# Regrouping the score matmuls and the PSUM banks of a two-block attention kernel

## The chip, the cores and the metric

The kernel runs on one core of a Trainium2 chip. The metric is the time of one execution on the device in microseconds (us). A core has a matrix engine (TensorE, PE in the profile; its weight loads are PEld), a vector engine (VectorE, DVE), a scalar engine (ScalarE, ACT), GpSimd (POOL) and a queue engine that starts DMAs (SyncE, SP). Matmuls write to PSUM, which has eight banks of 128 partitions by 512 fp32 values; VectorE and ScalarE read from there into SBUF.

## What is computed

Two independent attention blocks read two inputs of 2048 tokens by 640 features, and their outputs are put side by side. Both have 32 heads of 20 features.

```python
# A: sliding window of 256 tokens, softmax
scores = einsum("bhqd,bhkd->bhqk", q, k) * Dh**-0.5
scores = where((i - j >= 0) & (i - j < 256), scores, -1e9)
a = einsum("bhqk,bhkd->bhqd", softmax(scores), v) -> [B, S, D] @ wo
# B: linear attention, phi(t) = where(t > 0, t + 1, exp(t)) + 1e-6
kv = einsum("bhsd,bhse->bhde", phi(k), v); z = sum_s phi(k)
b = (phi(q) @ kv) / (phi(q) @ z + 1e-6) -> [B, S, D] @ wo
```

## The kernel before, in words

Tokens are cut into 16 blocks of 128 (NB). The framework tracks which instruction needs which tile, gives each tile a slot of its pool when an earlier tile of the same name has let go of it, and puts the instructions of each engine in an order ahead of time, in which work that is written later may be woven in where an engine would stand idle. Once that order is made, each engine keeps it: an instruction that waits holds back all behind it on its engine.

Up to about 115 us, x is loaded and transposed, and block B sums its key-value products over the token blocks (loop at line 131), in three PSUM banks of the pool `psB` (line 130). Then A's V, Q and K are projected (lines 200 to 237) and B's phi(q) (lines 238 to 261), in the four banks of `psAP`.

The attention loop of A (lines 288 to 359) takes the heads in eight groups g of four. The four heads lie on the partitions 0, 32, 64 and 96 of `qkg`, which DMAs fill (line 294). For each key block j of a group:

- Line 334: four score matmuls (20 rows of one head, 128 keys by up to 384 queries), each on its own 32 rows of the array (`tile_position`). Two share a tile `st` of two banks; the pool `psST` has two such tiles (line 277), so the second pair of j and the first pair of j+1 each wait until the exponential that reads the tile ahead of them is done.
- Line 341: one exponential on ScalarE for each pair, 128 by 2 x 384, from `st` into `e_t` in SBUF.
- Lines 345 and 351: GpSimd sets to zero what the causal diagonal and the window's edge exclude.
- `do_pv(j - 1)`, line 301: for each of the four heads up to three matmuls (line 308) of `e_t` with V into one PSUM tile `ops`, with one bank (`psO`, line 278); the column 21 of V is ones, so the softmax's denominator comes along. VectorE takes the reciprocal (line 316) and multiplies into `O_all` (line 317).

The second half of B (lines 417 to 472) is written behind this loop, and the framework weaves it in. For each of 16 token blocks tb: 10 matmuls of phi(q) with the masked key-value matrix into two tiles `na` and `nb` (line 422); on VectorE the denominators (lines 429, 434, 439) and two products (lines 442, 448); five transposes (line 457) and their copy (line 459); ten matmuls with B's output weights into `oa` (512 wide) and `ob` (128 wide; line 464), two copies (lines 470, 471) and a store. All take their tiles from the three banks of `psB`.

Last comes A's output projection (lines 475 to 494): for each token block five transposes of `O_all` (line 479), a copy on VectorE (line 481), ten matmuls (line 486), two copies on ScalarE (lines 492, 493) and a store. It too uses the three banks of `psB`.

So the banks of the attention loop are: three of `psB`, four of `psST`, one of `psO`.

Of the kernel before, what the change touches and what calls it, by code (L numbers as in the profile page):

```python
# [8 lines left out]
F32 = mybir.dt.float32  # L9
BF16 = mybir.dt.bfloat16  # L10
ALU = mybir.AluOpType
ACTF = mybir.ActivationFunctionType


@with_exitstack
def kernel(
# [110 lines left out]
    KVacc = bc1.tile([P, KVW], F32)  # L127
    nc.vector.memset(KVacc[:], 0.0)
    pqT_all = bc1.tile([P, KC, S], BF16)
    psB = ctx.enter_context(tc.tile_pool(name="psB", bufs=3, space=bass.MemoryType.PSUM))  # L130
    for tb in range(NB):
        kps = []
        for kk, (lo, hi) in enumerate([(0, 320), (320, 640)]):
            pb = psB.tile([P, 512], F32, name="pb")
# [21 lines left out]
        v1v = V1.rearrange("p (h e) -> p h e", e=E21)  # L156
        nc.gpsimd.memset(v1v[:, :, Dh:E21], 1.0)  # L157
        for (lo, hi, h0v, h1v) in [(0, 480, 0, 24), (480, 640, 24, 32)]:
            pb = psB.tile([P, 512], F32, name="pb")
# [11 lines left out]
        kva = psB.tile([P, 512], F32, name="pb")  # L171
        kvb = psB.tile([P, 512], F32, name="pb")
# [101 lines left out]
    epool = ctx.enter_context(tc.tile_pool(name="epool", bufs=6))  # L274
    smallp = ctx.enter_context(tc.tile_pool(name="smallp", bufs=3))
    lctx = ctx.enter_context(ExitStack())
    psST = lctx.enter_context(tc.tile_pool(name="psST", bufs=2, space=bass.MemoryType.PSUM, side="right"))
    psO = lctx.enter_context(tc.tile_pool(name="psO", bufs=1, space=bass.MemoryType.PSUM, side="right"))

    def repack_segments(col):  # L280
        c0, p0 = col // P, col % P
# [3 lines left out]
            segs.append((c0 + 1, 0, Dh - n1, n1))  # L285
        return segs

    for g in range(NG):
        qkg = awork.tile([P, 2, S], BF16)
        for t in range(2):  # L290
# [8 lines left out]
        e_tiles = {}  # L299

        def do_pv(i):
            ops = psO.tile([P, 4 * E21], F32, name="ops")
            kbs = [kb for kb in range(i - 2, i + 1) if kb >= 0]
            for s in range(4):
                h = 4 * g + s
                for ii, kb in enumerate(kbs):
                    part = i - kb
                    nc.tensor.matmul(  # L308
                        ops[:, s * E21:(s + 1) * E21],
                        lhsT=e_tiles[kb][:, s, part * P:(part + 1) * P],  # L310
                        rhs=V_aug[:, kb, h * E21:(h + 1) * E21],
                        start=(ii == 0), stop=(ii == len(kbs) - 1),
                    )
# [3 lines left out]
            nc.vector.tensor_tensor(  # L317
                out=O_all[:, i, 80 * g:80 * (g + 1)].rearrange("p (s d) -> p s d", d=Dh),
                in0=ops3[:, :, 0:Dh],
                in1=rden.to_broadcast([P, 4, Dh]),  # L320
                op=ALU.mult,
            )
            if i - 2 in e_tiles:
                del e_tiles[i - 2]

        for j in range(NB):
            nqb = min(3, NB - j)
            nq = nqb * P
            e_t = epool.tile([P, 4, 3 * P], BF16)
            for pair in range(2):  # L330
                st = psST.tile([P, 2, 512], F32)
                for sl in range(2):
                    s = 2 * pair + sl
                    nc.tensor.matmul(  # L334
                        st[:, sl, 0:nq],
                        lhsT=qkg[32 * s:32 * s + Dh, 1, j * P:(j + 1) * P],
                        rhs=qkg[32 * s:32 * s + Dh, 0, j * P:j * P + nq],
                        start=True, stop=True,
                        tile_position=(32 * s, 0),
                    )  # L340
                nc.scalar.activation(  # L341
                    out=e_t[:, 2 * pair:2 * pair + 2, 0:nq], in_=st[:, :, 0:nq],
                    func=ACTF.Exp, scale=scale,
                )
            nc.gpsimd.affine_select(  # L345
                out=e_t[:, :, 0:P], in_=e_t[:, :, 0:P],
                pattern=[[0, 4], [1, P]], compare_op=ALU.is_ge, fill=0.0,
# [65 lines left out]
    for idx, (ch, bank, c0, ncol) in enumerate(num_plan):  # L413
        first_of_bank.setdefault(bank, idx)
        last_of_bank[bank] = idx

    for tb in range(NB):
        na = psB.tile([P, 512], F32, name="pb")
        nb = psB.tile([P, 512], F32, name="pb")
        ntiles = (na, nb)  # L420
        for idx, (ch, bank, c0, ncol) in enumerate(num_plan):
            nc.tensor.matmul(  # L422
                ntiles[bank][:, c0:c0 + ncol],
                lhsT=pqT_all[:, ch, tb * P:(tb + 1) * P],
                rhs=KVbd[:, ch, 512 * bank + c0:512 * bank + c0 + ncol],
                start=(idx == first_of_bank[bank]), stop=(idx == last_of_bank[bank]),
            )
        den = bw2.tile([P, H, 1], F32)
        nc.vector.tensor_scalar(
            out=den[:, 0:24, :],  # L430
            in0=na[:, 0:24 * E21].rearrange("p (h e) -> p h e", e=E21)[:, :, Dh:E21],
            scalar1=1e-6, scalar2=None, op0=ALU.add,
        )
        nc.vector.tensor_scalar(
            out=den[:, 24:32, :],
            in0=nb[:, 0:8 * E21].rearrange("p (h e) -> p h e", e=E21)[:, :, Dh:E21],
            scalar1=1e-6, scalar2=None, op0=ALU.add,
        )
        nc.vector.reciprocal(out=den[:], in_=den[:])
        o_sb = bw2.tile([P, D], BF16)  # L440
        o_v = o_sb.rearrange("p (h d) -> p h d", d=Dh)
        nc.vector.tensor_tensor(
            out=o_v[:, 0:24, :],
            in0=na[:, 0:24 * E21].rearrange("p (h e) -> p h e", e=E21)[:, :, 0:Dh],
            in1=den[:, 0:24, :].to_broadcast([P, 24, Dh]),
            op=ALU.mult,
        )
        nc.vector.tensor_tensor(
            out=o_v[:, 24:32, :],
            in0=nb[:, 0:8 * E21].rearrange("p (h e) -> p h e", e=E21)[:, :, 0:Dh],  # L450
            in1=den[:, 24:32, :].to_broadcast([P, 8, Dh]),
            op=ALU.mult,
        )
        tpsb_t = psB.tile([P, 512], F32, name="pb")
        tpsb = tpsb_t[:].bitcast(BF16).rearrange("p (c t) -> p c t", t=P)
        for c in range(KC):
            nc.tensor.transpose(tpsb[:, c, :], o_sb[:, c * P:(c + 1) * P], ident[:])  # L457
        oTb = bw2.tile([P, KC, P], BF16)
        nc.vector.tensor_copy(out=oTb[:], in_=tpsb[:, 0:KC, :])
        oa = psB.tile([P, 512], F32, name="pb")  # L460
        ob = psB.tile([P, 512], F32, name="pb")
        for (tgt, lo, hi) in [(oa, 0, 512), (ob, 512, 640)]:
            for c in range(KC):
                nc.tensor.matmul(  # L464
                    tgt[:, 0:hi - lo],
                    lhsT=oTb[:, c, :], rhs=Wo_B[:, c, lo:hi],
                    start=(c == 0), stop=(c == KC - 1),
                )
        osbB = bw2.tile([P, D], BF16)
        nc.vector.tensor_copy(out=osbB[:, 0:512], in_=oa[:, 0:512])  # L470
        nc.vector.tensor_copy(out=osbB[:, 512:640], in_=ob[:, 0:128])
        nc.sync.dma_start(out2[tb * P:(tb + 1) * P, D:2 * D], osbB[:])

    lctx.close()
    for tb in range(NB):
        tpsA_t = psB.tile([P, 512], F32, name="pb")
        tpsA = tpsA_t[:].bitcast(BF16).rearrange("p (c t) -> p c t", t=P)
        for c in range(KC):
            nc.tensor.transpose(tpsA[:, c, :], O_all[:, tb, c * P:(c + 1) * P], ident[:])
        oT = awork.tile([P, KC, P], BF16)  # L480
        nc.vector.tensor_copy(out=oT[:], in_=tpsA[:, 0:KC, :])  # L481
        opa = psB.tile([P, 512], F32, name="pb")
        opb = psB.tile([P, 512], F32, name="pb")
        for (tgt, lo, hi) in [(opa, 0, 512), (opb, 512, 640)]:
            for c in range(KC):
                nc.tensor.matmul(  # L486
# [38 lines left out]
```

## Time and profile before

| | us |
|---|---|
| median of 6 runs | 481.14 (480.25 to 481.97) |
| the profiled execution: its time | 480.25 |
| its span, first to last instruction | 478.5 |
| TensorE busy in it | 418.9 |
| ScalarE busy in it | 246.8 |
| VectorE busy in it | 228.7 |
| GpSimd busy in it | 173.0 |

The profile is of one execution. Its second part cuts the span into 40 equal slices and gives the busy share of each engine in tenths, and under PEclk the clock that TensorE was granted, in tenths of full speed. A list of groups gives, for the instructions of one line and form, the count, then the busy time and the mean of one in ns, then the time for which the engine had stood idle just before them and what ended it. The chain of waits goes back from the last instruction, at each step to what released it. Tables by stretch give, for each engine, the busy time and the number of instructions.

### The profile page before, as it was taken

How to read it: one execution, taken by the hardware profiler on the slowest of the kernel's cores; microseconds unless marked ns; L12 is line 12 of the kernel's file. 1: busy time of each engine (PE TensorE's matmuls, PEld its weight loads, DVE VectorE, ACT ScalarE, POOL GpSimd, SP SyncE). 2: the span in 40 equal slices, each digit the busy share in tenths (PEclk: the TensorE clock that was granted, in tenths of full speed). 3: DMA queues.
4: the chain of work that ended last, by engine and by line, in shares of the span. 5: the costliest groups of instructions: out<-in, count | busy, mean ns of one | idle time of the engine just before them, and what ended most of it. 6: DMA issues, size and time to landing. Idle time of an engine off the chain costs nothing.

```text
span 478.5 us, 9156 instructions
## 1 busy us (share of the span) xinstructions
PE 418.9 (88%) x3580; PEld 217.4 (45%) x3612; DVE 228.7 (48%) x635; ACT 246.8 (52%) x377; POOL 173.0 (36%) x373
## 2 busy tenths in 40 slices
PE   2299999999999495999999999999999988899775
PEld 1166666655444132444445444444444434344443
DVE  1188889887333489444444444344344422222221
ACT  0012222222223134776777777777777788777332
POOL 0010000000003920654555655656555567555000
PEclk9999999999999879555555555555555555555899
DMA  8980000000001300002102003012020020000111
GB/s 299 366 322 2 1 0 1 2 0 2 0 1 30 80 1 0 15 15 53 32 15 55 29 15 71 16 29 56 15 55 16 15 70 3 1 15 0 70 70 69
DMA packets 14154, 22.86 MB, mean 48 GB/s; under 512 B 1440, under 2 KB 11552, under 8 KB 14112
## 3 DMA queue, kind: packets, MB, share of 16 engines
q1 hardware_dynamic: 10688, 17.21, 12.2%
q10 hardware_dynamic: 3424, 5.08, 3.0%
q8 instruction: 28, 0.46, 0.4%
q14 instruction: 14, 0.11, 0.1%
HBM read 11.80 MB, written 5.24 MB: 36 GB/s over the span
## 4 chain that ended last, share of the span: by engine, by line
PE 70%; DVE 9%; ACT 8%; POOL 5%; DMA 4%; issue 3%; SPq 1%; ACTq 0%; POOLq 0%; DVEq 0%
PE st L334 17%; PE pb L464 9%; PE aps L226 9%; PE ops L308 8%; ACT e_t L341 7%; PE pb L486 5%; PE pb L136 5%; DMA Wv_A<-in_A_wqkv_dram 4%; PE aps L204 4%; PE pb L161 4%; PE pb L422 2%; PE pb L457 2%; DVE pqT_all L258 2%; DVE pqT_all L254 2%; PE pb L176 2%
## 5 line engine op out<-in xcount | busy, mean ns | idle before, releaser
L341 ACT ACTIVATE e_t<-st 128x768 bf16<-128x768 f32 (+2 forms) x256 | 191.6, 769 | 61.9 <-PE st L334 53.6
L334 PE MATMUL st<-qkg 20*128 20x384 bf16 (+2 forms) x512 | 121.9, 473 | 14.6 <-ACT e_t L341 5.0
L345 POOL TENSOR_SCALAR_AFFINE_SELECT e_t<-e_t 128x512 bf16<-128x512 bf16 x128 | 81.2, 634 | 126.1 <-ACT e_t L341 126.1
L308 PEld LDWEIGHTS <-e_t 128*128 128x128 bf16 x1440 | 60.0, 108 | 48.3 <-issue 29.7
L316 DVE RECIPROCAL rden<-ops 128x4 f32<-128x4 f32 x128 | 23.0, 180 | 115.0 <-PE ops L308 114.5
L308 PE MATMUL ops<-V_aug,e_t 128*128 128x21 bf16 x1440 | 73.3, 184 | 4.2 <-POOL e_t L351 0.9
L351 POOL TENSOR_SCALAR_AFFINE_SELECT e_t<-e_t 128x512 bf16<-128x512 bf16 x112 | 71.0, 634 | 0.0
L334 PEld LDWEIGHTS <-qkg 20*128 20x128 bf16 x512 | 27.2, 99 | 56.7 <-issue 49.5
L464 PE MATMUL pb<-Wo_B,oTb 128*128 128x512 bf16 (+1 forms) x144 | 49.8, 436 | 0.6 <-DVE O_all L317 0.3
L226 PE MATMUL aps<-xT_A,Wqk_u 128*128 128x512 bf16 x193 | 44.9, 379 | 0.4
L204 PE MATMUL aps<-Wv_A,xT_A 128*128 128x480 bf16 (+1 forms) x160 | 30.8, 305 | 9.5 <-DMA Wv_A<-in_A_wqkv_dram 8.9
L486 PE MATMUL pb<-Wo_A,oT 128*128 128x512 bf16 (+1 forms) x153 | 30.5, 330 | 7.7 <-DVE oT L481 7.3
L317 DVE TENSOR_TENSOR O_all<-ops,rden 128x80 bf16<-128x80 f32 x128 | 30.6, 239 | 3.8
L244 PE MATMUL aps<-xT_B,Wb 128*128 128x512 bf16 x98 | 26.3, 420 | 6.2 <-DVE pqT_all L254 6.0
L236 ACT CAST qkT_u<-aps 128x512 bf16<-128x512 f32 x20 | 11.7, 585 | 37.3 <-DVE qkT_u L234 37.3
L157 POOL MEMSET V<- 128x32 bf16 x16 | 3.7, 244 | 71.6 <-PE pb L176 58.3
L226 PEld LDWEIGHTS <-Wqk_u 128*128 128x128 bf16 x200 | 19.4, 98 | 21.1
L136 PE MATMUL pb<-Wb,xT_B 128*128 128x320 bf16 x160 | 26.2, 298 | 0.0
L147 ACT ACTIVATE ek<-pb 128x320 bf16<-128x320 f32 x32 | 14.0, 437 | 21.9 <-PE pb L136 21.5
L234 DVE CAST qkT_u<-aps 128x512 bf16<-128x512 f32 x20 | 13.8, 690 | 23.1 <-PE aps L226 23.1
L161 PE MATMUL pb<-Wb,xT_B 128*128 128x480 bf16 (+1 forms) x160 | 24.3, 299 | 0.0
L252 ACT ACTIVATE eqc<-aps 128x512 bf16<-128x512 f32 x20 | 11.9, 597 | 23.9 <-DVE pqT_all L254 16.1
(55 smaller groups left out, 410.4 us busy)
## 6 DMA issues: line engine op xcount, KB each, us to landing
qkg<-qkT_u SPq DMA_DIRECT2D x56, 80.0 KB
x_nat_A<-in_A_x_dram SPq DMA_DIRECT2D x4, 640.0 KB
x_nat_B<-in_B_x_dram ACTq DMA_DIRECT2D x4, 640.0 KB
out_dram<-osbB SPq DMA_DIRECT2D x16, 160.0 KB
out_dram<-osb SPq DMA_DIRECT2D x16, 160.0 KB
Wb<-in_B_wqkv_dram SPq DMA_DIRECT2D x1, 2400.0 KB
Wqk_u<-in_A_wqkv_dram ACTq DMA_DIRECT2D x1, 1600.0 KB
Wv_A<-in_A_wqkv_dram SPq DMA_DIRECT2D x1, 800.0 KB
```

The costliest lines, as they stand in the source:

```text
L136: nc.tensor.matmul(pb[:, 0:hi - lo], lhsT=xT_B[:, kc, tb * P:(tb + 1) * P], rhs=Wb[:, kc, D + lo:D + hi], start=(kc == 0), stop=(kc == KC ...
L161: nc.tensor.matmul(pb[:, 0:hi - lo], lhsT=xT_B[:, kc, tb * P:(tb + 1) * P], rhs=Wb[:, kc, 2 * D + lo:2 * D + hi], start=(kc == 0), stop=(k ...
L204: nc.tensor.matmul(vps[:, bank, 0:hi - lo], lhsT=xT_A[:, kc, kb * P:(kb + 1) * P], rhs=Wv_A[:, kc, lo:hi], start=(kc == 0), stop=(kc == KC ...
L226: nc.tensor.matmul(qps[:, k, 0:tn], lhsT=Wqk_u[:, kc, c * P:(c + 1) * P], rhs=xT_A[:, kc, ts0:ts0 + tn], start=(kc == 0), stop=(kc == KC - 1),
L308: nc.tensor.matmul(ops[:, s * E21:(s + 1) * E21], lhsT=e_tiles[kb][:, s, part * P:(part + 1) * P], rhs=V_aug[:, kb, h * E21:(h + 1) * E21] ...
L317: nc.vector.tensor_tensor(out=O_all[:, i, 80 * g:80 * (g + 1)].rearrange("p (s d) -> p s d", d=Dh), in0=ops3[:, :, 0:Dh], in1=rden.to_broa ...
L334: nc.tensor.matmul(st[:, sl, 0:nq], lhsT=qkg[32 * s:32 * s + Dh, 1, j * P:(j + 1) * P], rhs=qkg[32 * s:32 * s + Dh, 0, j * P:j * P + nq], ...
L341: nc.scalar.activation(out=e_t[:, 2 * pair:2 * pair + 2, 0:nq], in_=st[:, :, 0:nq], func=ACTF.Exp, scale=scale,)
L345: nc.gpsimd.affine_select(out=e_t[:, :, 0:P], in_=e_t[:, :, 0:P], pattern=[[0, 4], [1, P]], compare_op=ALU.is_ge, fill=0.0, base=0, channe ...
L351: nc.gpsimd.affine_select(out=e_t[:, :, 2 * P:3 * P], in_=e_t[:, :, 2 * P:3 * P], pattern=[[0, 4], [-1, P]], compare_op=ALU.is_gt, fill=0. ...
L464: nc.tensor.matmul(tgt[:, 0:hi - lo], lhsT=oTb[:, c, :], rhs=Wo_B[:, c, lo:hi], start=(c == 0), stop=(c == KC - 1),)
L486: nc.tensor.matmul(tgt[:, 0:hi - lo], lhsT=oT[:, c, :], rhs=Wo_A[:, c, lo:hi], start=(c == 0), stop=(c == KC - 1),)
```

## The change

The change regroups the attention loop and hands its eight PSUM banks out in another way:

- The score tiles become three (six banks). The two tiles of a key block are taken together and all four score matmuls are written one after the other, ahead of the two exponentials. A dependency by hand makes the first of the four wait for the first exponential of the key block before (`DEP_SYNC`); `DEP_ORDER` is defined and not used.
- `do_pv` runs two key blocks behind the scores, where it was one. Its output tile is a slot of a ring of four (`opsring`), all within one bank.
- The second half of B has one bank instead of three: the two parts of the numerators, the transposes and the two parts of the output projection each take it in turn and are evicted before the next. The reciprocal is taken for each part of the heads by itself, so there are two for each token block.
- B's first half keeps three banks, in a pool of its own that is released ahead of the attention loop.
- A's output projection gets banks of its own: four for the results, two for the transposes, in the place of the score tiles.

```diff
-    psB = ctx.enter_context(tc.tile_pool(name="psB", bufs=3, space=bass.MemoryType.PSUM))
+    psB1 = tc.alloc_tile_pool(name="psB1", bufs=3, space=bass.MemoryType.PSUM)
...
+    psB1.release()
+    psB = ctx.enter_context(tc.tile_pool(name="psB", bufs=1, space=bass.MemoryType.PSUM))
+    psO = ctx.enter_context(tc.tile_pool(name="psO", bufs=1, space=bass.MemoryType.PSUM))
...
-    psST = lctx.enter_context(tc.tile_pool(name="psST", bufs=2, space=bass.MemoryType.PSUM, side="right"))
-    psO = lctx.enter_context(tc.tile_pool(name="psO", bufs=1, space=bass.MemoryType.PSUM, side="right"))
+    psST = lctx.enter_context(tc.tile_pool(name="psST", bufs=3, space=bass.MemoryType.PSUM, side="right"))
...
+    opsring = psO.tile([P, 4, 4 * E21], F32)
+    first_exp = []
...
-            ops = psO.tile([P, 4 * E21], F32, name="ops")
+            ops = opsring[:, i % 4, :]
...
+            sts = [psST.tile([P, 2, 512], F32, name="st"), psST.tile([P, 2, 512], F32, name="st")]
+            for s in range(4):
+                mm = nc.tensor.matmul(
+                    sts[s // 2][:, s % 2, 0:nq],
+                    lhsT=qkg[32 * s:32 * s + Dh, 1, j * P:(j + 1) * P],
+                    rhs=qkg[32 * s:32 * s + Dh, 0, j * P:j * P + nq],
+                    start=True, stop=True,
+                    tile_position=(32 * s, 0),
+                )
+                if s == 0 and first_exp:
+                    tc.add_manual_dep(mm.ins, first_exp[-1].ins.name, DEP_SYNC, reason="four")
             for pair in range(2):
-                st = psST.tile([P, 2, 512], F32)
-                for sl in range(2):
-                    s = 2 * pair + sl
-                    nc.tensor.matmul(
...
+                ex = nc.scalar.activation(
+                    out=e_t[:, 2 * pair:2 * pair + 2, 0:nq], in_=sts[pair][:, :, 0:nq],
                     func=ACTF.Exp, scale=scale,
                 )
+                if pair == 0:
+                    first_exp.append(ex)
...
-            if j >= 1:
-                do_pv(j - 1)
+            if j >= 2:
+                do_pv(j - 2)
+        do_pv(NB - 2)
         do_pv(NB - 1)
...
+        for bank, (hlo, hhi) in enumerate([(0, 24), (24, 32)]):
+            nt = psB.tile([P, 512], F32, name="pb")
...
+            nc.vector.reciprocal(out=den[:, hlo:hhi, :], in_=den[:, hlo:hhi, :])
...
+        for (lo, hi) in [(0, 512), (512, 640)]:
+            opt = psB.tile([P, 512], F32, name="pb")
...
+            nc.vector.tensor_copy(out=osbB[:, lo:hi], in_=opt[:, 0:hi - lo])
...
     lctx.close()
+    psAO = ctx.enter_context(tc.tile_pool(name="psAO", bufs=4, space=bass.MemoryType.PSUM, side="right"))
+    psAT = ctx.enter_context(tc.tile_pool(name="psAT", bufs=2, space=bass.MemoryType.PSUM, side="right"))
     for tb in range(NB):
-        tpsA_t = psB.tile([P, 512], F32, name="pb")
+        tpsA_t = psAT.tile([P, 512], F32, name="pat")
...
-        opa = psB.tile([P, 512], F32, name="pb")
-        opb = psB.tile([P, 512], F32, name="pb")
+        opa = psAO.tile([P, 512], F32, name="pao")
+        opb = psAO.tile([P, 512], F32, name="pao")
```

More of the change, by code (lines that the diff above doesn't have):

```diff
@@ L12 @@
 ACTF = mybir.ActivationFunctionType
+DEP_SYNC = mybir.DependencyInfo(mybir.DependencyClass.Sync, mybir.DependencyReason.DATA)
+DEP_ORDER = mybir.DependencyInfo(mybir.DependencyClass.NoSync, mybir.DependencyReason.DATA)
 @with_exitstack
@@ L133 @@
         for kk, (lo, hi) in enumerate([(0, 320), (320, 640)]):
-            pb = psB.tile([P, 512], F32, name="pb")
+            pb = psB1.tile([P, 512], F32, name="pb")
             for kc in range(KC):
@@ L158 @@
         for (lo, hi, h0v, h1v) in [(0, 480, 0, 24), (480, 640, 24, 32)]:
-            pb = psB.tile([P, 512], F32, name="pb")
+            pb = psB1.tile([P, 512], F32, name="pb")
             for kc in range(KC):
@@ L170 @@
             )
-        kva = psB.tile([P, 512], F32, name="pb")
-        kvb = psB.tile([P, 512], F32, name="pb")
+        kva = psB1.tile([P, 512], F32, name="pb")
+        kvb = psB1.tile([P, 512], F32, name="pb")
         for ch, (h0, h1) in enumerate(chunk_heads):
@@ L329 @@
             e_t = epool.tile([P, 4, 3 * P], BF16)
-            for pair in range(2):
-                st = psST.tile([P, 2, 512], F32)
-                for sl in range(2):
-                    s = 2 * pair + sl
[L334 to L342, printed above, removed]
+            sts = [psST.tile([P, 2, 512], F32, name="st"), psST.tile([P, 2, 512], F32, name="st")]
[9 more added lines that the diff above has]
+                    tc.add_manual_dep(mm.ins, first_exp[-1].ins.name, DEP_SYNC, reason="four")
+            for pair in range(2):
+                ex = nc.scalar.activation(
+                    out=e_t[:, 2 * pair:2 * pair + 2, 0:nq], in_=sts[pair][:, :, 0:nq],
                     func=ACTF.Exp, scale=scale,
                 )
+                if pair == 0:
+                    first_exp.append(ex)
             nc.gpsimd.affine_select(
@@ L417 @@
     for tb in range(NB):
[L418 to L427, printed above, removed]
@@ L428 @@
-        den = bw2.tile([P, H, 1], F32)
[L429 to L439, printed above, removed]
+        den = bw2.tile([P, H, 1], F32)
@@ L440 @@
         o_sb = bw2.tile([P, D], BF16)
         o_v = o_sb.rearrange("p (h d) -> p h d", d=Dh)
[L442 to L453, printed above, removed]
+        for bank, (hlo, hhi) in enumerate([(0, 24), (24, 32)]):
+            nt = psB.tile([P, 512], F32, name="pb")
+            for idx, (ch, bk, c0, ncol) in enumerate(num_plan):
+                if bk != bank:
+                    continue
+                nc.tensor.matmul(
+                    nt[:, c0:c0 + ncol],
+                    lhsT=pqT_all[:, ch, tb * P:(tb + 1) * P],
+                    rhs=KVbd[:, ch, 512 * bank + c0:512 * bank + c0 + ncol],
+                    start=(idx == first_of_bank[bank]), stop=(idx == last_of_bank[bank]),
+                )
+            nh = hhi - hlo
+            nc.vector.tensor_scalar(
+                out=den[:, hlo:hhi, :],
+                in0=nt[:, 0:nh * E21].rearrange("p (h e) -> p h e", e=E21)[:, :, Dh:E21],
+                scalar1=1e-6, scalar2=None, op0=ALU.add,
+            )
+            nc.vector.reciprocal(out=den[:, hlo:hhi, :], in_=den[:, hlo:hhi, :])
+            nc.vector.tensor_tensor(
+                out=o_v[:, hlo:hhi, :],
+                in0=nt[:, 0:nh * E21].rearrange("p (h e) -> p h e", e=E21)[:, :, 0:Dh],
+                in1=den[:, hlo:hhi, :].to_broadcast([P, nh, Dh]),
+                op=ALU.mult,
+            )
@@ L459 @@
         nc.vector.tensor_copy(out=oTb[:], in_=tpsb[:, 0:KC, :])
-        oa = psB.tile([P, 512], F32, name="pb")
-        ob = psB.tile([P, 512], F32, name="pb")
-        for (tgt, lo, hi) in [(oa, 0, 512), (ob, 512, 640)]:
+        osbB = bw2.tile([P, D], BF16)
+        for (lo, hi) in [(0, 512), (512, 640)]:
+            opt = psB.tile([P, 512], F32, name="pb")
             for c in range(KC):
                 nc.tensor.matmul(
-                    tgt[:, 0:hi - lo],
+                    opt[:, 0:hi - lo],
                     lhsT=oTb[:, c, :], rhs=Wo_B[:, c, lo:hi],
@@ L468 @@
                 )
-        osbB = bw2.tile([P, D], BF16)
-        nc.vector.tensor_copy(out=osbB[:, 0:512], in_=oa[:, 0:512])
-        nc.vector.tensor_copy(out=osbB[:, 512:640], in_=ob[:, 0:128])
+            nc.vector.tensor_copy(out=osbB[:, lo:hi], in_=opt[:, 0:hi - lo])
         nc.sync.dma_start(out2[tb * P:(tb + 1) * P, D:2 * D], osbB[:])
     lctx.close()
+    psAO = ctx.enter_context(tc.tile_pool(name="psAO", bufs=4, space=bass.MemoryType.PSUM, side="right"))
+    psAT = ctx.enter_context(tc.tile_pool(name="psAT", bufs=2, space=bass.MemoryType.PSUM, side="right"))
     for tb in range(NB):
-        tpsA_t = psB.tile([P, 512], F32, name="pb")
+        tpsA_t = psAT.tile([P, 512], F32, name="pat")
         tpsA = tpsA_t[:].bitcast(BF16).rearrange("p (c t) -> p c t", t=P)
```

## The prediction

> **What bounds the kernel now.** I read the page first (engine shares, slices, clock), then the stretches of the attention loop, then the chain of waits inside it, then its instructions in order of time.
>
> ```profile
> span 478.5 us, 9156 instructions
> ...
> PE   2299999999999495999999999999999988899775
> ...
> ACT  0012222222223134776777777777777788777332
> ...
> PEclk9999999999999879555555555555555555555899
> ```
>
> From the 17th slice to the 37th TensorE is full or nearly so while its granted clock is half, and ScalarE stands mostly at seven tenths. That is the attention loop; the stretches below begin with its first exponential and end with its last. Columns: PE busy, PEld busy, DVE, ACT, POOL, clock, DMA share, GB/s.
>
> ```profile
> 180.00:190.00 10.00, 5.79 (x33) 2.60 (x32) 9.90 (x20) 3.58 (x6) 0.00 (x0) 1.00 0.00 0
> 190.10:388.00 197.90, 186.82 (x1852) 90.65 (x1868) 83.81 (x318) 148.25 (x197) 111.83 (x183) 0.50 0.13 34
> 388.00:410.00 22.00, 18.98 (x207) 8.60 (x205) 5.51 (x26) 19.50 (x28) 16.04 (x28) 0.50 0.05 12
> 410.00:442.80 32.80, 30.26 (x299) 14.37 (x301) 8.38 (x36) 25.13 (x37) 18.25 (x30) 0.50 0.02 8
> 442.80:478.50 35.70, 24.63 (x204) 14.21 (x204) 7.01 (x17) 10.40 (x28) 0.63 (x1) 0.95 0.19 68
> ACT e_t L341 <- PE st L334: 53.6, 119, 1.4
> ```
>
> The loop takes 252.7 us (442.8 - 190.1). Up to 388, block B's second half is woven in and TensorE is busy 94% of the time; ScalarE waits 53.6 us in all for score matmuls. From 388 to 410, with no filler, ScalarE is nearly full: there another limit shows. The chain of waits gives the price of each TensorE step at half clock (start, length, what):
>
> ```profile
> 205.84 0.16 PE ops L308 x2
> 206.00 0.43 PE pb L464
> 206.43 0.26 PE ops L308 x10
> 206.69 0.43 PE st L334 x2
> ...
> 208.26 0.22 PE pb L464 x2
> ...
> 209.61 0.14 PE pb L422 x2
> ...
> 210.34 0.27 PE pb L422 x3
> ...
> 211.30 0.38 PE pb L422 x5
> ...
> 213.51 0.66 PE pb L457 x5
> ```
>
> One key block j costs TensorE two pairs of score matmuls, 2 x 0.43, and twelve PV matmuls, 0.16 + 0.26: about 1.29. One token block of B costs L422 0.14 + 0.27 + 0.38 = 0.79, L457 0.66, L464 5 x 0.43 + 5 x 0.11 = 2.70: 4.15. So 128 x 1.29 + 16 x 4.15 = 231 us of the 252.7; the first pieces of A's output projection (410 to 442.8) and waits are the rest. TensorE bounds the loop.
>
> ScalarE's own need comes from the stretch without filler and from the shapes:
>
> ```profile
> 390.95 1.52 ACT e_t L341 x2
> ...
> 392.59 0.65 POOL e_t L345
> ...
> 393.28 0.44 PE ops L308 x10
> 393.73 0.45 PE st L334 x2
> ...
> 394.28 1.52 ACT e_t L341 x2
> L341 ACT ACTIVATE e_t<-st 128x768 bf16<-128x768 f32 x224 | 176.5, 809 | 53.9 <-PE st L334 45.9 <-DVE pqT_all L258 2.1 <-ACT e_t L341 0.3
> L341 ACT ACTIVATE e_t<-st 128x512 bf16<-128x512 f32 x16 | 9.4, 597 | 3.6 <-PE st L334 3.6
> L341 ACT ACTIVATE e_t<-st 128x256 bf16<-128x256 f32 x16 | 5.8, 382 | 4.4 <-PE st L334 4.1
> ```
>
> Two wide exponentials back to back take 1.52, so 112 x 1.52 + 9.4 + 5.8 = 185 us is the floor that ScalarE sets. Here the ring is exp, GpSimd mask, PV, scores, exp: 3.33 us (394.28 - 390.95) for two key blocks, because PV of block j-1, queued ahead of the next scores, waits for a mask just being made.
>
> **The change, part by part.** *Four score matmuls together.* Three score tiles instead of two let all four matmuls of a key block go once the first exponential of the block before is done. Each uses its own 32 rows of the array and its own bank.
>
> ```profile
> 188.86 0.34 PE L334 MATMUL st<-qkg 20*128 20x384 bf16 x4 [3.06 <-issue]
> ```
>
> At the loop's start both tiles were free and four did run together: 0.34 us for all, at the full clock of the stretch 180 to 190. At half clock a pair costs 0.43; four cost between 0.43 (as a pair) and 0.86 (as two pairs). I take 0.45, by this row. Gain on TensorE: up to 128 x 0.41 = 52 us. TensorE's need falls to 128 x (0.45 + 0.42) + 66 = 178 us, below ScalarE's 185.
>
> The price is a wait: the first score matmul of j stands until the first exponential of j-1 ends, and in TensorE's order the other three, PV and B's next step stand behind it; the exponentials of j wait for it. It fits barely: a score batch of 0.45 and two hand-overs between engines must go under the second exponential's 0.76. So ScalarE runs without a gap only if TensorE arrives on time: per key block it has 1.52 - 0.45 - 0.42 = 0.65 us for B's work. Two 512-wide L464 matmuls, which is what the order before puts in a block, need 0.86: 0.21 too much in some 40 blocks, 8.4 us. L457 (0.66) and L422 (0.79) overrun by 0.01 and 0.14 in 16 blocks each, 2.4 us: together 11.
>
> *PV two blocks behind instead of one.* No PV waits for a fresh mask any more: the ring above breaks, and 1.66 per block can fall to 1.52. Six e_t buffers hold the five blocks alive. The ring of four output slots lies in one bank, in which PV of i+1 follows the division of i by more than a block: nothing either way.
>
> *B's second half with one bank instead of three.* Work is the same but for one more reciprocal per token block (16 x at most 0.35), covered by VectorE's idle time (83.81 busy of 197.9). But the five steps now alternate: matmuls, eviction, matmuls in the same bank. That wait isn't in the trace. The evictions:
>
> ```profile
> L442 DVE TENSOR_TENSOR o_sb<-pb,den 128x480 bf16<-128x480 f32 x16 | 10.5, 657 | 0.4
> L448 DVE TENSOR_TENSOR o_sb<-pb,den 128x160 bf16<-128x160 f32 x16 | 4.8, 299 | 0.0
> L459 DVE COPY oTb<-pb 128x640 bf16<-128x640 bf16 x16 | 7.9, 492 | 11.1 <-PE pb L457 11.0
> L470 DVE CAST osbB<-pb 128x512 bf16<-128x512 f32 x16 | 11.1, 692 | 10.2 <-PE pb L464 10.0 <-PE ops L308 0.3
> L471 DVE CAST osbB<-pb 128x128 bf16<-128x128 f32 x16 | 4.7, 292 | 6.8 <-PE pb L464 6.8
> PE st L334 <- DVE O_all L317: 4.7, 10, 0.5
> ```
>
> Where scores and PV lie between two steps, about 0.9 us, most evictions are hidden: price 0 (or slightly below: less filler per block). If TensorE stands for each, 2.43 per token block and hand-overs, about 1 us for each of 80 steps. With three banks TensorE's largest wait for VectorE in the loop was 4.7 us in all; nearest to that, I take 0.1 x 80 = 8.
>
> *A's output projection with its own banks.* It takes the score tiles' banks, so it can't start before the last exponential; before, its first blocks ran inside the loop.
>
> ```profile
> 447.21 1.53 PE pb L486 x10
> 448.74 0.29 PE pb L479 x5
> 449.03 0.02 issue
> 449.06 0.50 DVE oT L481
> 449.56 0.05 issue
> ...
> 474.92 0.58 ACT osb L492
> ```
>
> A round was 2.40 (1.53 + 0.29 + 0.57 of copy and hand-overs). With two transpose banks the next block's transposes fill the copy: between 1.82 and 2.40; I take 1.82. Sixteen rounds are 29.1, about 1.6 more for the first at half clock, and 3.6 from the last copy to the span's end: 34.3, against 35.7 now. At 2.40 it is 43.6.
>
> *The rest*, the renamed pool of B's first pass, keeps three banks: nothing.
>
> **Sum**, against the profiled execution: 190.1 before the loop, unchanged; loop 185 + 11 + 8 + 2 (an estimate for the first fill and the group ends) = 206; tail 34.3; span 430.4; 1.75 around the span (480.25 - 478.5): 432.2. The median of the runs is 0.9 above the profiled run, so 433.
>
> A rule of the Trainium skill, "TensorE: Matmul & The Clock Gate", part 1, says that the array goes to full clock after about 3.4 us of sustained activity. The trace differs: 0.50 for 198 us with TensorE busy 94%. By the rule every TensorE price here would halve, as in the third rival.
>
> **The rivals.** *The four don't gather.* The wait is put on the first of the four alone; the second needs only the tile. If TensorE's order puts that one ahead, or splits the batch otherwise, a block again costs 0.86 for scores: loop 231 + about 10 of waits = 241, total 190.1 + 241 + 34.3 + 1.75 + 0.9 = 468. For it: nothing in the trace shows an order with this wait; against: four did go together at 188.86.
>
> *The one bank stops TensorE*, the way to slower. Without these stalls the loop is 198; the change breaks even at a loop of 254, so from 0.7 us per step on, 56 / 80, it loses. At 1 us per step: 198 + 80 = 278, total 505. For it: evictions of 0.3 to 0.7 us behind VectorE's own PV work, on an engine that keeps order. Against: VectorE is idle more than half the loop.
>
> *The clock rises*, since the four use all row groups at once: the loop goes to ScalarE's 185 + 2, total 414. Against: dense 128-row L464 work in the loop didn't lift it.
>
> *B isn't done when the loop ends.* B took 198 us for 16 blocks with three banks; at a slower pace, five blocks are left, 5 x 2.1 us at full clock beside A's projection: about 11 more, 444.
>
> **How the numbers follow.** Forecast 57%, not gathered 18%, stopped by the bank 9%, clock 5%, B left over 11%. The forecast's own bounds: bank stalls 0 to 0.3 per step and tail at 2.40 give 425 to 458; a thinner spread of B's filler takes up to 8 off, 417. The range 414 to 468 takes in the clock, B left over and half of "not gathered". Faster by over 0.2%, about what a measurement here can tell, holds in the forecast, the clock, B left over and most of "not gathered": 0.87; slower 0.10; same 0.03.
>
> **What would show it.** Right: score matmuls in fours with about 0.45 from one step to the next; the loop near 206 us with ScalarE's waits for st under 20 us; rounds of A's projection near 1.8. Wrong: scores in pairs or one by three; TensorE waiting for VectorE's evictions for tens of us; L464 after the last exponential; a clock other than 0.50 in the loop.

## The result and the profile after

The changed kernel takes 425.99 us (median of 8 runs, 424.31 to 427.07). The kernel before, measured beside it, takes 481.73 us (median of 16, 480.0 to 482.91). The ratio is 0.8847, with a 95% interval of 0.8831 to 0.8863: some 56 us less, where the prediction had 48. The profiled execution of the changed kernel took 426.39 us, its span 424.7.

The page of the changed kernel, with the span, the busy tenths of TensorE and ScalarE and the granted clock over 40 slices:

```profile
span 424.7 us, 9174 instructions
...
PE   2279999999999995868898888888988888887996
...
ACT  0002221222222222339989799899989999896443
...
PEclk9999999999999996985555555556555555555999
```

The two have changed places: in the loop ScalarE now stands at nine tenths and TensorE mostly at eight, at the same half clock. The same in numbers: the loop (first exponential to last), the tail behind it, and a stretch inside the loop. Columns as in the prediction: start:end and length, then PE, PEld, DVE, ACT, POOL busy, clock, DMA share, GB/s.

```profile
190.80:388.70 197.90, 169.55 (x2298) 88.61 (x2311) 98.47 (x390) 181.09 (x256) 145.68 (x239) 0.51 0.14 35
388.70:424.70 36.00, 29.71 (x259) 18.34 (x263) 7.95 (x21) 12.06 (x32) 0.84 (x2) 0.93 0.20 74
290.00:310.00 20.00, 16.84 (x242) 9.04 (x241) 10.89 (x44) 18.64 (x27) 15.14 (x26) 0.59 0.21 51
```

The loop took 252.7 us before and takes 197.9 now; ahead of it lie 190.1 and 190.8, behind it 35.7 and 36.0. All of the gain is in the loop. The waits of it (engine and line waiting, what for: us in total, times, longest):

```profile
PE st L339 <- ACT e_t L349: 17.9, 47, 0.6
ACT e_t L349 <- PE st L339: 13.8, 34, 1.5
PE pb L465 <- DVE osbB L470: 3.4, 14, 0.4
PE pb L436 <- DVE o_sb L449: 1.9, 8, 0.4
```

ScalarE waits 13.8 us for scores, where it was 53.6. TensorE now waits 17.9 us for ScalarE, which is the wait put in by hand, and only 3.4 and 1.9 us for VectorE to empty B's one bank. The 17.9 are too much: 15 of the 160 matmuls of line L465 have no record in this trace, and their time counts as idle. The run with the plain output tile below has the same order in its loop and all 160 records; there this wait is 12.7 us, and TensorE is busy 175.75 us of 198.0 instead of 169.55.

TensorE's instructions in order of time near the end of the loop, and two rows of ScalarE's (start, length, engine and line, operation, count; in brackets idle time before and who ended it), show the new rhythm. One record of a 512-wide matmul at 373 is missing from the trace; its weight load is there, so the gap before 374.11 holds two of them, and the idle 0.36 in that row is none.

```profile
372.38 0.51 PE L339 MATMUL st<-qkg 20*128 20x384 bf16 x4
372.82 0.50 PE L315 MATMUL opsring<-V_aug,e_t 128*128 128x21 bf16 x12
...
374.11 0.51 PE L339 MATMUL st<-qkg 20*128 20x384 bf16 x4 [0.36 <-ACT e_t L349]
374.55 0.49 PE L315 MATMUL opsring<-V_aug,e_t 128*128 128x21 bf16 x12
374.73 1.51 ACT L349 ACTIVATE e_t<-st 128x768 bf16<-128x768 f32 x2 [0.24 <-PE st L339]
374.89 1.01 PE L465 MATMUL pb<-Wo_B,oTb 128*128 128x512 bf16 x2
375.84 0.51 PE L339 MATMUL st<-qkg 20*128 20x384 bf16 x4
...
376.46 12.18 ACT L349 ACTIVATE e_t<-st 128x768 bf16<-128x768 f32 x18 [0.21 <-PE st L339]
376.62 0.59 PE L465 MATMUL pb<-Wo_B,oTb 128*128 128x512 bf16 x1
377.32 0.51 PE L339 MATMUL st<-qkg 20*128 20x384 bf16 x4
377.99 0.48 PE L465 MATMUL pb<-Wo_B,oTb 128*128 128x128 bf16 x3 [0.15 <-DVE osbB L470]
...
380.42 0.51 PE L339 MATMUL st<-qkg 20*128 20x384 bf16 x4 [0.42 <-ACT e_t L349]
...
381.91 0.51 PE L339 MATMUL st<-qkg 20*128 20x384 bf16 x4 [0.56 <-ACT e_t L349]
...
383.40 0.51 PE L339 MATMUL st<-qkg 20*128 20x384 bf16 x4 [0.56 <-ACT e_t L349]
```

Four score matmuls, twelve PV matmuls, a piece of B, again and again. Without a piece of B a block takes 1.49 us (380.42, 381.91, 383.40), and TensorE waits 0.42 to 0.56 of it for ScalarE. With one 512-wide matmul it takes 1.48 (375.84 to 377.32), with two 1.73 (374.11 to 375.84). So a lump (pieces of B that stand together in one gap) of two sticks out by 0.24, and ScalarE then has to wait: 0.24 and 0.21 at 374.73 and 376.46. At 377.99 the 128-wide matmuls wait 0.15 until VectorE has emptied the one bank.

### The profile page after: what moved, and what is told of

Same layout as the page of the kernel before. It is cut to its first block, busy times and chain, and to the rows that moved or that the text cites. A ratio compares the mean times of both kernels' runs of the same rounds, so it can differ in the third digit from the quotient of the medians.

```text
span 424.7 us, 9174 instructions
## 1 busy us (share of the span) xinstructions
PE 358.4 (84%) x3583; PEld 197.5 (46%) x3612; DVE 230.2 (54%) x651; ACT 236.7 (56%) x377; POOL 172.8 (41%) x373
## 4 chain that ended last, share of the span: by engine, by line
PE 52%; ACT 21%; DVE 9%; POOL 6%; DMA 5%; issue 4%; SPq 2%; ACTq 0%; POOLq 0%; DVEq 0%
ACT e_t L349 20%; PE aps L229 10%; PE pb L465 7%; PE st L339 7%; DMA Wb<-in_B_wqkv_dram 5%; PE pao L487 5%; PE opsring L315 5%; PE pb L139 5%; PE pb L164 4%; PE aps L207 4%; DVE osbB L470 2%; PE pb L179 2%; POOL kvmask L380 2%; DVE pqT_all L261 2%; POOL kvmask L384 2%
## 5 line engine op out<-in xcount | busy, mean ns | idle before, releaser
L349 ACT ACTIVATE e_t<-st 128x768 bf16<-128x768 f32 (+2 forms) x256 | 181.1, 768 | 18.5 <-PE st L339 13.8
L339 PE MATMUL st<-qkg 20*128 20x384 bf16 (+2 forms) x512 | 63.4, 473 | 22.9 <-ACT e_t L349 17.9
L315 PEld LDWEIGHTS <-e_t 128*128 128x128 bf16 x1440 | 52.6, 106 | 36.5 <-issue 31.8
L323 DVE RECIPROCAL rden<-opsring 128x4 f32<-128x4 f32 x128 | 23.2, 181 | 83.6 <-PE opsring L315 83.3
L315 PE MATMUL opsring<-V_aug,e_t 128*128 128x21 bf16 x1440 | 62.3, 182 | 2.5 <-DVE O_all L324 0.8
L465 PE MATMUL pb<-Wo_B,oTb 128*128 128x128 bf16 (+1 forms) x145 | 48.6, 429 | 4.3 <-DVE osbB L470 3.4
L339 PEld LDWEIGHTS <-qkg 20*128 20x128 bf16 x512 | 14.4, 99 | 61.8 <-ACT e_t L349 56.6
L324 DVE TENSOR_TENSOR O_all<-opsring,rden 128x80 bf16<-128x80 f32 x128 | 30.5, 238 | 3.2
L237 DVE CAST qkT_u<-aps 128x512 bf16<-128x512 f32 x20 | 13.8, 690 | 23.1 <-PE aps L229 23.1
L487 PE MATMUL pao<-Wo_A,oT 128*128 128x128 bf16 (+1 forms) x155 | 23.9, 307 | 2.4 <-DVE oT L482 2.1
```

What stands on the lines that cost most here:

```text
L315: nc.tensor.matmul(ops[:, s * E21:(s + 1) * E21], lhsT=e_tiles[kb][:, s, part * P:(part + 1) * P], rhs=V_aug[:, kb, h * E21:(h + 1) * E21] ...
L324: nc.vector.tensor_tensor(out=O_all[:, i, 80 * g:80 * (g + 1)].rearrange("p (s d) -> p s d", d=Dh), in0=ops3[:, :, 0:Dh], in1=rden.to_broa ...
L339: mm = nc.tensor.matmul(sts[s // 2][:, s % 2, 0:nq], lhsT=qkg[32 * s:32 * s + Dh, 1, j * P:(j + 1) * P], rhs=qkg[32 * s:32 * s + Dh, 0, j ...
L349: ex = nc.scalar.activation(out=e_t[:, 2 * pair:2 * pair + 2, 0:nq], in_=sts[pair][:, :, 0:nq], func=ACTF.Exp, scale=scale,)
L465: nc.tensor.matmul(opt[:, 0:hi - lo], lhsT=oTb[:, c, :], rhs=Wo_B[:, c, lo:hi], start=(c == 0), stop=(c == KC - 1),)
L487: nc.tensor.matmul(tgt[:, 0:hi - lo], lhsT=oT[:, c, :], rhs=Wo_A[:, c, lo:hi], start=(c == 0), stop=(c == KC - 1),)
```

## The experiments

The theory was: the gain comes from the fours, which the wait by hand holds together, and the PV step two blocks behind lets ScalarE run through; what is left above ScalarE's floor is B's lumps and the one bank. The rivals were that the wait is not needed, that the longer lag or the freed banks do the work, or that the bank costs more than the lumps. Ratios are to the kernel before, with their 95% intervals.

**Without the wait by hand.**

```diff
-                if s == 0 and first_exp:
-                    tc.add_manual_dep(mm.ins, first_exp[-1].ins.name, DEP_SYNC, reason="four")
```

> The changed kernel without the wait by hand on the first of the four score matmuls; three score tiles stay. In its instruction order the scores then stand in pairs nearly everywhere, since a pair may go as soon as its own tile is free. Theory (TensorE time is what the four save: a batch of four costs 0.43 us like a pair): TensorE pays 2 x 0.43 per key block again, the loop goes from 198 us back to about 232 and the time to about 460 us. Rival (the third score tile itself, by letting scores run ahead, brings the gain): at most 432 us.

Measured: 464.55 us, 0.9646 [0.9614, 0.9678], 38.6 us more than with the wait. The loop, in the same columns, and what ScalarE waits for:

```profile
190.70:426.70 236.00, 228.60 (x2312) 104.74 (x2312) 100.17 (x389) 188.44 (x256) 146.81 (x239) 0.50 0.12 29
```

```profile
ACT e_t L347 <- PE st L339: 42.0, 91, 1.7
```

TensorE is full again, 228.60 of 236.00, and ScalarE waits 42.0 us. In TensorE's order of instructions the scores stand in pairs: each pair goes as soon as its tile is free. With the wait, 125 of 128 key blocks have their four in one piece. Three tiles alone don't gather the four; the wait does.

**The lag taken back.**

```diff
-            if j >= 2:
-                do_pv(j - 2)
-        do_pv(NB - 2)
+            if j >= 1:
+                do_pv(j - 1)
         do_pv(NB - 1)
```

> The changed kernel with PV one key block behind the scores, as before, instead of two; fours stay. Theory A (TensorE's time alone decides): its need stays at 178 us, under ScalarE's 185, so the time stays within 426 to 434 us. Theory B (with fours the lag is needed): in each block PV of j-1 stands in TensorE's order ahead of the scores of j+1 and waits for the mask after the second exponential: 0.76 + 0.1 + 0.65 + 0.44 makes a ring of about 1.95 us instead of 1.5, 112 x 0.45 = 50 us more, 470 to 476 us.

Measured: 447.03 us, 0.9283 [0.9252, 0.9314]; loop 219.5. That lies between the theories. Behind the last filler, its instructions in order of time (ScalarE's and TensorE's lines):

```profile
388.14 3.08 ACT L349 ACTIVATE e_t<-st 128x768 bf16<-128x768 f32 x4 [0.17 <-PE st L339]
...
390.48 0.44 PE L315 MATMUL opsring<-V_aug,e_t 128*128 128x21 bf16 x10 [0.56 <-POOL e_t L355]
390.85 0.51 PE L339 MATMUL st<-qkg 20*128 20x384 bf16 x4
...
391.45 3.08 ACT L349 ACTIVATE e_t<-st 128x768 bf16<-128x768 f32 x4 [0.23 <-PE st L339]
...
394.78 0.81 ACT L349 ACTIVATE e_t<-st 128x768 bf16<-128x768 f32 x1 [0.24 <-PE st L339]
```

The ring of exponential, mask, PV and scores is there: PV waits 0.56 for a mask, the scores stand behind it, and ScalarE waits 0.2 for them. Two blocks take 391.45 - 388.14 = 3.31 and 394.78 - 391.45 = 3.33, the 3.33 of the kernel before. Against 1.49 this is 0.17 more for each block, and 112 x 0.17 = 19 us; measured were 21 (447.03 - 425.99). That the whole loop pays by this ring isn't shown: it is read from the stretch without filler. While B is woven in, the order is more broken, too: 22 score batches are split here, where the change has 3, and TensorE's waits for masks come to 12.2 us in all. In this stretch the ring is no worse because the scores of one more block stand ahead of the waiting PV, so the ring closes over two blocks and not over one.

**Pairs, with all else of the change.**

```diff
-    psST = lctx.enter_context(tc.tile_pool(name="psST", bufs=3, space=bass.MemoryType.PSUM, side="right"))
+    psST = lctx.enter_context(tc.tile_pool(name="psST", bufs=2, space=bass.MemoryType.PSUM, side="right"))
...
+            for pair in range(2):
+                st = psST.tile([P, 2, 512], F32)
+                for sl in range(2):
+                    s = 2 * pair + sl
+                    nc.tensor.matmul(
...
```

> The changed kernel with the pair loop and the two score tiles of the kernel before; two banks stand empty; the lag of two, B's single bank and the projection's own banks stay. Theory (fours carry the gain): loop about 235 to 240, 463 to 470 us. Rival (lag and projection carry it): below 440 us. If B's single bank costs much where TensorE is the bound, it shows here: above 481 us.

**The lag alone, in the kernel before.**

```diff
-            if j >= 1:
-                do_pv(j - 1)
+            if j >= 2:
+                do_pv(j - 2)
+        do_pv(NB - 2)
         do_pv(NB - 1)
```

> The kernel before with nothing changed but PV two key blocks behind the scores. Theory (TensorE bounds the loop while B is woven in): only the stretch without filler gains, about 20 blocks x 0.15 = 3 us, so 474 to 479 us. Rival (the ring through the mask bounds the loop): 445 us or less.

Measured: pairs 466.8 us, 0.9692 [0.9659, 0.9725]; the lag alone 477.08, 0.9913 [0.9882, 0.9944]. Their loops, first of the pairs, then of the lag alone:

```profile
191.00:431.20 240.20, 231.79 (x2338) 108.45 (x2336) 99.54 (x392) 191.53 (x256) 146.76 (x239) 0.50 0.12 29
```

```profile
190.90:436.10 245.20, 240.15 (x2346) 109.45 (x2347) 94.89 (x378) 192.29 (x259) 146.63 (x239) 0.50 0.11 28
```

Without the fours TensorE is full in both, so a shorter ring has little to give: the lag is worth 4.1 us in the kernel before (481.15, measured beside it, to 477.08) and 21 us with the fours (447.03 to 425.99). The fours are worth 41 us with the lag (466.8 to 425.99). Each part opens the way for the other. Pairs with all the rest of the change are 10 us faster than the lag alone: 5.0 in the loop (245.2 to 240.2) and 5.5 behind it (39.1 to 33.6). So B's one bank costs nothing visible there, where TensorE is the limit; which part of the rest saves these 10 us wasn't separated.

**B's second half left out.** Its loop only stores one tile of zeros 16 times.

```diff
-        for bank, (hlo, hhi) in enumerate([(0, 24), (24, 32)]):
...
-            nc.vector.tensor_copy(out=osbB[:, lo:hi], in_=opt[:, 0:hi - lo])
+    osbB = bw2.tile([P, D], BF16)
+    nc.vector.memset(osbB[:], 0.0)
```

> The changed kernel without B's second half: its numerators, divisions, transposes and output projection are left out, and zeros are stored in their place. Theory (ScalarE bounds the loop, B's filler costs what sticks out): the loop falls from 198 us to 8 x (14 x 1.49 + 1.7) = 180 to 184 us, time 410 to 414 us. Rival (TensorE's order or the score hand-over bounds the loop also without filler): 420 us or more.

Measured: 414.99 us, 0.8621 [0.8585, 0.8656].

```profile
189.40:376.90 187.50, 123.05 (x1924) 65.86 (x1925) 53.30 (x252) 179.90 (x256) 145.74 (x239) 0.50 0.11 23
```

187.5 us is ScalarE's floor, with the first fill and the ends and starts of groups; the prediction had 185 + 2. The loop expected for this run, 180 to 184, was too short, and the time lies 1 us above its range: ScalarE is busy 179.90 us and idle 7.6, nearly all of it in the first blocks of each group, for which the expectation had nothing. So weaving in all of B costs the loop 197.9 - 187.5 = 10.4 us, where 11 and 8 had been set for lumps and bank. By the order of TensorE's instructions, two 512-wide matmuls of L465 stand in one gap 29 times, and three more gaps are as long: 32 x 0.24 = 7.7 us of the 10.4 by the spacing read above.

The trace of the changed kernel also allows a count at ScalarE, from the start of one key block's first exponential to the next one's. The 32 blocks behind these gaps lie 7.9 us above 1.49 in all. About another 2.0 us lie at the sixteen blocks with four or five of the 128-wide matmuls, as at 377.99: that is the bank. Ahead of 42 blocks inside the groups stands no piece of B or a short one (one matmul, or the three for the last eight heads), and there ScalarE has no idle time at all; so the hand-over from ScalarE to TensorE and back costs nothing by itself.

**Every eviction of B done twice.**

```diff
-            nc.vector.tensor_copy(out=osbB[:, lo:hi], in_=opt[:, 0:hi - lo])
+            for _ in range(2):
+                nc.vector.tensor_copy(out=osbB[:, lo:hi], in_=opt[:, 0:hi - lo])
```

(the same for the copy to `oTb` and the product into `o_sb`)

> The changed kernel with each of B's evictions from its single bank done twice (the two products, the copy of the transposes, the two output copies), so that the bank is held 2.4 us longer per token block, 39 us in all. Theory (the hand-overs of the single bank lie under scores and PV): 2 to 10 us more, 428 to 436 us. Rival (TensorE stands for the evictions): the 39 us come through, 460 us or more.

Measured: 429.19 us, 0.8905 [0.8868, 0.8943], 3.2 us more than the change. Loop and tail, and B's projection as it stands in the tail's groups (count, then busy and mean ns, then idle before):

```profile
191.60:387.40 195.80, 166.73 (x2245) 86.46 (x2260) 117.23 (x437) 180.80 (x256) 146.21 (x239) 0.50 0.13 33
387.40:427.90 40.50, 33.41 (x316) 20.72 (x319) 20.07 (x53) 12.10 (x32) 0.64 (x1) 1.00 0.21 78
```

```profile
L472 PE MATMUL pb<-Wo_B,oTb 128*128 128x128 bf16 (+1 forms) x27 | 5.0, 308 | 0.6 <-DVE osbB L478 0.6
```

VectorE is busy 31 us more by the two stretches (117.23 + 20.07 against 98.47 + 7.95), and the loop is no longer for it: 195.8. Instead B falls behind, and 27 matmuls of its projection come in the tail, which grows from 36.0 to 40.5. A sixth of the projection has thus left the loop, so the price of the longer evictions is the 3.2 us of the whole, and not read from the loop alone. The rival by which B is left over appears here in small; the one by which the bank stops TensorE does not.

**One transpose bank for A's projection.**

```diff
-    psAT = ctx.enter_context(tc.tile_pool(name="psAT", bufs=2, space=bass.MemoryType.PSUM, side="right"))
+    psAT = ctx.enter_context(tc.tile_pool(name="psAT", bufs=1, space=bass.MemoryType.PSUM, side="right"))
```

> The changed kernel with one transpose bank in A's output projection instead of two. Theory: each round waits for its copy again, 2.40 us instead of 1.87, 16 x 0.53 = 8 us more, 433 to 435 us. Rival (TensorE is full in the tail, or the copies of the results set the pace): at most 428 us.

**The next block's transposes written ahead of this block's matmuls.**

```diff
+    oT_next = a_transposed(0)
     for tb in range(NB):
+        oT = oT_next
+        if tb + 1 < NB:
+            oT_next = a_transposed(tb + 1)
```

> The changed kernel with the transposes of A's output projection written one token block ahead of its matmuls, so that the copy of the next block lies under the matmuls of this one. Now TensorE waits about 0.55 us after every second block. Theory: 7 x 0.5 = 3 to 4 us less, 422 to 423 us. Rival (the store or ScalarE's copies set the end): no change.

Measured: 434.6 us, 0.9023 [0.8985, 0.906], for one bank, and 422.0 us, 0.8762 [0.8735, 0.8788], for the transposes ahead. The chains of waits in the tail (start, length, what): the changed kernel, then one bank, then transposes ahead.

```profile
395.00 0.29 PE pat L480 x5
...
395.32 0.50 DVE oT L482
...
395.87 1.75 PE pao L487 x11
...
398.76 0.29 PE pat L480 x5
```

```profile
399.81 0.50 DVE oT L482
...
400.36 1.53 PE pao L487 x10
401.89 0.29 PE pat L480 x5
402.21 0.50 DVE oT L482
```

```profile
396.46 0.28 PE pat L480 x5
396.74 1.36 PE pao L494 x10
398.10 0.28 PE pat L480 x5
398.38 1.36 PE pao L494 x10
```

With one bank every round has the copy in it: 402.21 - 399.81 = 2.40, as before. In the changed kernel the copy is on the chain only in every second round: two rounds take 398.76 - 395.00 = 3.76, so 1.88 each. Written ahead, it is never there, and a round is 1.64. The version with transposes ahead is 4.0 us faster than the change, and the fastest of the kernels here that compute everything.

**Smaller lumps.** B's projection in two halves of 320 columns, alone and with the transposes ahead:

```diff
-        for (lo, hi) in [(0, 512), (512, 640)]:
+        for (lo, hi) in [(0, 320), (320, 640)]:
```

> The changed kernel with B's output projection cut into 320 and 320 columns instead of 512 and 128. TensorE's time is the same; two matmuls in a gap take 0.53 instead of 0.86 us and no longer stick out of the 0.6 us that a block leaves. Theory (the lumps cost the loop): 5 to 9 us less, 417 to 421 us. Rival (the order of the program spreads B otherwise, or the single bank's waits are what costs): no change, 425 to 428 us.

> Both of the edits before together. Theory: the loop and the tail add, 414 to 418 us. If either edit brings nothing, the time is that of the other.

Measured: 426.74 us, 0.8862 [0.8839, 0.8885], alone, and 423.7, 0.8792 [0.877, 0.8814], with the transposes ahead, against 422.0 without the halves: nothing gained, and both expectations (417 to 421, 414 to 418) were missed. In the order of instructions the framework now puts four of the smaller matmuls into 25 gaps and three into 7, so the lumps stay as long. Counted at ScalarE as above, the 25 blocks behind four lie 10.0 us above 1.49.

**The filler dealt out by hand**, with halves and transposes ahead: seven pieces for each token block of B, one for each key block, each held behind that block's scores by a dependency of order only. The other three score matmuls are tied behind the first, and the masked key-value matrix is made ready ahead of the loop.

```diff
+            if j < NB - 1:
+                next(b_order, None)
```

> The kernel of the tail edit, with B's second half put in place by hand: its output projection in halves of 320 columns, its work cut into seven pieces per token block (numerators 24 heads, numerators 8 heads, transposes, then 3, 2, 3 and 2 matmuls of the projection), one piece per key block, each tied by an order dependency behind the score matmuls of its key block; the three other score matmuls are tied behind the first. No piece is longer than 0.8 us. Theory (what the loop lost against the 187.5 us without B are lumps of filler over 0.6 us): 24 pieces stick out by 0.18 and 13 key blocks have their scores split, the loop is 190 to 195 us instead of 197, 415 to 420 us in all. Rival (the waits of the single bank or the splits of the scores are what costs): 422 us or more.

Measured: 427.04 us, 0.8863 [0.8835, 0.8891]. The loop, then a split score batch in order of time (TensorE's and ScalarE's lines), then a piece of three in the chain of waits:

```profile
190.80:392.60 201.80, 185.62 (x2325) 90.51 (x2323) 103.59 (x396) 181.59 (x256) 146.10 (x239) 0.50 0.14 34
```

```profile
249.89 0.49 PE L460 MATMUL st<-qkg 20*128 20x384 bf16 x1 [0.55 <-ACT e_t L476]
250.32 0.34 PE L362 MATMUL pb<-KVbd,pqT_all 128*128 128x42 bf16 x3
250.59 0.50 PE L460 MATMUL st<-qkg 20*128 20x384 bf16 x3
...
251.21 3.09 ACT L476 ACTIVATE e_t<-st 128x768 bf16<-128x768 f32 x4 [0.67 <-PE st L460]
```

```profile
253.10 0.81 PE pb L395 x3
```

The expected 415 to 420 us were missed. The loop became longer, 201.8 against 198.6 with halves and transposes ahead alone (196.8 with the transposes ahead and no halves). A piece of three matmuls still takes 0.81, over the 0.65 that the prediction allowed. And 18 score batches are split in the trace, 15 into one and three and 3 into two and two, where the change has 3 split in all; each split is one more step of about 0.44 for TensorE, and after the one shown ScalarE waits 0.67. Counted at ScalarE, 30 blocks behind three matmuls lie 5.0 us above 1.49, blocks behind two of them nothing, and the 16 split ones that don't begin a group 9.7 us. So the lumps are most of the 10.4 us, but this deal is no remedy: the splits cost more than the shorter lumps gave.

**The ring of output slots taken back.**

```diff
-            ops = opsring[:, i % 4, :]
+            ops = psO.tile([P, 4 * E21], F32, name="ops")
```

> The changed kernel with PV's output as one plain tile again instead of a slot of the ring of four. Theory (the division of one key block is long done when the next PV starts, so the ring brings nothing): 425 to 428 us. Rival (the ring lets PV run ahead of the divisions): 432 us or more.

Measured: 425.68 us, 0.8846 [0.8825, 0.8867]: the ring does nothing. In this run, with one transpose bank and with the transposes ahead, the loop has the same fours and the same pieces of B in its gaps as in the change, and its length in the four traces is 196.7 to 198.1 us. So lengths of the loop, and the 10.4 us above, are good to about 1 us.

## Why the prediction was right, and which terms were mis-sized

The mechanism was right: TensorE's load falls below ScalarE's, and ScalarE sets the loop. Point by point:

- **Fours.** They gather in 125 of 128 blocks, and a batch takes one step. This row of the changed kernel's chain of waits has it, 253.48 to 253.92:

```profile
253.48 0.44 PE st L339 x4
253.92 0.43 PE opsring L315 x12
```

  0.44 was measured where 0.45 had been set; the other bound, 0.86, is what the kernels with pairs pay. The row that 0.45 was taken by (0.34 for four, at full clock) shows that four go together, and not what a batch costs at half clock. That it costs what a pair does was a good guess.
- **ScalarE's floor.** 187 predicted, 187.5 measured without B. That the two agree so closely is luck: the work, set at 185, took 179.9, and the idle time, set at 2, was 7.6.
- **B in the loop.** This is the term that was mis-sized: 11 for lumps and 8 for the bank, 10.4 measured for both. The lumps came near: 7.7 by count and spacing, 7.9 by ScalarE's steps, where 8.4 stood for the 512-wide ones. The bank's part was too dear. The 0.1 for each of 80 steps, taken from the waits before, is paid at sixteen of them, the 128-wide matmuls behind the copy of the 512-wide part, with 2.0 us in all. The other evictions lie nearly all under the scores and PV, as "price 0" had it: TensorE's waits for VectorE there come to 5.3 us in the whole loop (3.4 + 1.9), and doubling every eviction cost 3.2 us. The two smaller overruns, for which 2.4 had been set, show about 0.5 by the same count.
- **Loop in sum.** 206 predicted, 197.9 measured. The 7 us by which the time was too high are these 8.1, less 1.7 in the tail and 0.7 ahead of the loop, and 1.3 because the median lies 0.4 below the profiled execution here and was set 0.9 above.
- **Tail.** 34.3 predicted, 36.0 measured. Sixteen rounds of 1.88 for 1.82 are 1.0 of the 1.7. The copy was taken as hidden in every round; it is hidden in every second one. The other 0.7 comes from the clock of this one execution: the kernel with the plain output tile has the same rounds and a tail of 35.4, its granted clock was 0.93 in the three us from 391 to 394, and at the same place of the tail (392 to 395) it was 0.73 in the changed kernel.
- **Lag.** "1.66 per block can fall to 1.52" held: 1.49. It had no price of its own in the sum; with the fours it is worth 21 us.
- **Rivals.** "The four don't gather" is what happens without the wait: 464.55 measured, 468 worked out. "The one bank stops TensorE" would have needed 0.7 us for each step, and did not come. "B left over" came only with doubled evictions. "The clock rises" did not come: the loop's clock is 0.51, with 0.59 in one stretch. The rule of the Trainium skill, "TensorE: Matmul & The Clock Gate", part 1, that was weighed there does not describe this loop: with TensorE busy 169.55 of 197.90 us the clock stays near half.

## What to carry to other kernels

When an engine is full of small steps at a price for each step, look for steps that can run side by side, and give the scheduler a reason to keep them together: a free buffer alone let it run them as they came (464.55 against 425.99 us). Then look for what is late next, since the second limit (here the ring through the mask) hid behind the first and was worth almost nothing until the first had gone. Filler in a loop that another engine paces costs where a piece is longer than its gap, and not by its sum (175.75 - 123.05 = 53 us of TensorE's busy time, by the loop with all records and the one without B, cost 10 here). One bank between two engines was enough for it here, where other work lies between most of its steps.

## What the runs showed of the hardware

- Four score matmuls on the four row groups of the array take as long at half clock as two: 0.44 from the start of a batch to TensorE's next step, against 0.43 for a pair.
- Where no filler is in the way, two wide exponentials take 1.49 from the start of the first to the start of the next two (382.53 - 381.04), a little under the 1.52 that was read before from start to end:

```profile
381.04 1.44 ACT e_t L349 x2
...
382.53 1.45 ACT e_t L349 x2
```

- The clock rose to 0.59 for a stretch of the loop (290 to 310 us in the changed kernel) while the mean was 0.51. No run here shows why.
